# Chunk attention, top-1 MoE and a swish MLP on one core: the MoE's up-projection with its weights as the stationary operand

## The chip, the core and the metric

The kernel runs on one core of one Trainium2 chip. The engines named below are TensorE (PE, its weight loads PEld), VectorE (DVE), ScalarE (ACT), GpSimd (POOL) and SyncE (SP), which here only issues DMAs. The metric is the time of one execution on the device in microseconds (us).

## What is computed

Attention in chunks of 64, then a mixture of 8 experts in which each token goes to one, then an MLP with a swish, for 4608 tokens of width 512:

```python
def _moe_ref(x, expert_emb, tau, w1, w2):         # x [4608, 512], w1 [8, 512, 1024], w2 [8, 1024, 512]
    ...
    for e in range(E):
        mask = expert_idx == e
        ...
        h = np.maximum(x[mask] @ w1[e], 0.0)
        out[mask] = gate_w[mask, None] * (h @ w2[e])

def reference(**kwargs):
    ...
    attn_out = _attn_ref(**attn_kwargs)
    B, H, S, D = attn_out.shape
    x = np.ascontiguousarray(attn_out.transpose(0, 2, 1, 3)).reshape(B * S, H * D)
    x = _moe_ref(x=x, **moe_kwargs)
    return _moe2_ref(x=x, **moe2_kwargs)
```

The change is in the line `h = ...`: how that product is laid on PE.

## The kernel before

Three stages follow each other. The first makes attention and the router's logits for 36 tiles of 128 tokens (to about 250 us). The second sorts the tokens by expert and runs the experts over 39 tiles of at most 128 tokens of one expert each (235 to 760 us). The third is the MLP (from 764 us).

**Numbers in halves.** x, w1, h and w2 are held as a high and a low half in float16; a product takes three matmuls (high x high, high x low, low x high). w1H and w1L, w2H and w2L are the halves of the current expert's weights.

**One tile i of the expert stage.** `find(i)` and `fetch(i)` (POOL) gather the tokens' rows into xg; `turn(i)` (L867, SP) turns them with a DMA transpose into xTm: 8 blocks of 128 x 128, 4 high and 4 low, with the model's width on the partitions. `mm1(i)` is the up-projection: for each of the 4 blocks c along the width three products, each over two PSUM banks ph of 512 columns. A matmul takes a block of xTm as the stationary operand (128 x 128, loaded by a LDWEIGHTS) and moves 512 columns of w1 past it (L879): 24 matmuls, and h comes out with the tokens on the partitions. `mm1_evac(i)` then makes the two halves of h: Relu on ACT (L887), the difference on DVE (L888), one pair per bank. h has one buffer (L884). A DMA transpose on SP's queue (L892) turns h into hT, 16 blocks of 128 x 128. `mm2(i)` takes the blocks of hT as stationary operand and moves w2 (L916): 24 matmuls of 512 columns into py. `mm2_evac(i)` squares, scales and splits py on ACT and DVE (L929 to L946) and POOL scatters it to ys (L950).

**The order.** Engines run their instructions in the order of the code. In the loop over tiles 3 to 38 an iteration i is: mm1(i), turn(i+2), fetch(i+3), find(i+4), swap(i+1, 1), the matmuls of mm2(i-1), swap(i, 2), the evacuation of mm2(i-1), and one step of `dec`. So on PE mm1(i) is followed by mm2(i-1), then mm1(i+1), then mm2(i).

**swap(i, which)** (L831) is a branch on ACT and DVE that is taken where tile i is the first of an expert: four calls of `w_split` (L773), each 1024 columns, make the halves of w1 (which = 1) or w2 (which = 2) out of the staging buffers stg or stgB: ACT makes the high half (L781), DVE the low one (L786). Then SP loads the next expert's weights.

**dec** is work for the third stage that runs beside the experts: 32 blocks of w_in and w_out are loaded, decoded from float64 by ACT and four DVE instructions (up to L1166) and split by ACT (L1109) and POOL (L1110); the 16 blocks of w_in also go through sums on POOL (L1118), of which ACT's copies wait.

Of the kernel before, what the change touches and what calls it, by code (L numbers as in the profile page):

```python
# [9 lines left out]
F32 = mybir.dt.float32  # L10
F16 = mybir.dt.float16
# [3 lines left out]
AF = mybir.ActivationFunctionType  # L15
ALU = mybir.AluOpType
# [18 lines left out]
def kernel(  # L35
# [13 lines left out]
    nc = tc.nc  # L49
# [3 lines left out]
    FF = w1.shape[2]  # L53
# [3 lines left out]
    KD = DM // 128  # L57
    KF = FF // 128
# [28 lines left out]
    w1H, w1L = w1HL[:, 0], w1HL[:, 1]  # L87
# [55 lines left out]
    for t in vt:  # L143
# [15 lines left out]
        out=tri16, in_=ones16, pattern=[[1, 128]], compare_op=ALU.is_gt, fill=0.0,  # L159
# [116 lines left out]
    def steps(n):  # L276

        paused.clear()
        while n > 0 and todo:
            try:  # L280
                n -= 1
                if next(todo[0]) == "found":
                    return
            except StopIteration:
                todo.popleft()
# [147 lines left out]
    def evac_XT(t):  # L433
        xT = att.tile([128, 2 * KD, 128], F16, tag="xTa", name="xTa", bufs=2)
        xv = xT.rearrange("p (a c) k -> p a c k", a=2)
        if t >= 30:
            nc.scalar.activation(out=xv, in_=xtp, func=AF.Copy)
        else:
            nc.vector.tensor_copy(xv, xtp)  # L439
        xT_t[t] = xT  # L440
# [59 lines left out]
    def scat():  # L500
        if scats and scats[0][0] < now[0]:
            scats.popleft()[1]()
# [270 lines left out]
    def w_split(which, c, n, eng, st=stg):  # L773

        hlf, o = divmod(c * n, 2048)
        _, H_, L_ = WL[which]
        flat = slice(c * n, (c + 1) * n)
        H_ = H_.rearrange("p a f -> p (a f)")[:, flat]
        L_ = L_.rearrange("p a f -> p (a f)")[:, flat]
        src = st[hlf][:, o:o + n]  # L780
        nc.scalar.activation(out=H_, in_=src, func=AF.Copy, scale=2.0 ** W_EXP)  # L781
        if eng is nc.gpsimd:
            eng.tensor_tensor(out=src, in0=src, in1=w_pow.to_broadcast([128, n]), op=ALU.mult)
            eng.tensor_tensor(out=L_, in0=src, in1=H_, op=ALU.subtract)
        else:
            eng.scalar_tensor_tensor(  # L786
                out=L_, in0=src, scalar=2.0 ** W_EXP, in1=H_, op0=ALU.mult, op1=ALU.subtract
            )
# [19 lines left out]
    def first_split(n):  # L808
        for _ in range(n):
            c = fs_n[0]  # L810
            fs_n[0] += 1
            w_split(c // 8 + 1, c % 8, 512, (nc.vector, nc.gpsimd)[c % 2])
# [18 lines left out]
    def swap(i, which):  # L831

        if which == 1:
            flag[i] = reg(fl_i[0:1, i:i + 1], [ENG.Activation, ENG.DVE], 1)
        with tc.If(flag[i] > 0):
            for c in range(4):
                w_split(which, c, 1024, nc.vector, stage[which])
        load_next(i, which)


    mt_t, xg_t, xTm_t, hT_t = {}, {}, {}, {}
# [27 lines left out]

    ph_t = {}  # L870

    def mm1_part(i, c):
        xT = xTm_t[i]
        if c == 0:
            ph_t[i] = [ps.tile([128, 512], F32, tag="A", name="ph", bufs=2) for _ in range(2)]
        p = ph_t[i]
        for a, wt, st, sp in ((c, w1H, c == 0, False), (c, w1L, False, False), (KD + c, w1H, False, c == KD - 1)):
            for f in range(2):
                nc.tensor.matmul(p[f], xT[:, a, :], wt[:, c, f * 512:(f + 1) * 512], start=st, stop=sp)  # L879

    def mm1_evac(i):
        xTm_t.pop(i)
        p = ph_t.pop(i)
        h = mo.tile([128, 2, FF], F16, tag="h", name="h", bufs=1)  # L884
        for f in range(2):
            cc = slice(f * 512, (f + 1) * 512)
            nc.scalar.activation(out=h[:, 0, cc], in_=p[f], func=AF.Relu)  # L887
            nc.vector.scalar_tensor_tensor(  # L888
                out=h[:, 1, cc], in0=p[f], scalar=0.0, in1=h[:, 0, cc], op0=ALU.max, op1=ALU.subtract
            )  # L890
        hT = mo.tile([128, 2 * KF, 128], F16, tag="hT", name="hT", bufs=2)
        nc.sync.dma_start_transpose(hT, h.rearrange("p a f -> p (a f)"))  # L892
        hT_t[i] = hT

    def mm1(i):
        for c in range(KD):
            mm1_part(i, c)
        mm1_evac(i)

    py_t = {}  # L900

# [85 lines left out]
    for n in range(NTILE + 3):  # L987
# [46 lines left out]
        if n >= NTILE:  # L1034
            drip(6)
            mm1_part(0, n - NTILE)
    mm1_part(0, 3)
    now[0] = 2 * NTILE
    scat()
    mm1_evac(0)  # L1040
    evac_XT(NTILE - 1)
    steps(20)
    mm1_part(1, 0)
# [12 lines left out]
    while scats:  # L1056
        scat()
    mm1_part(1, 3)
    mm1_evac(1)
    steps(99)  # L1060
    find(3)
    mm2(0)
    mm1(2)
    fetch(3)
    turn(3)
# [37 lines left out]
    def big_split():  # L1103
# [3 lines left out]

        def low(f, H_, L_):
            nc.scalar.activation(out=H_, in_=f, func=AF.Copy)  # L1109
            nc.gpsimd.tensor_tensor(out=L_, in0=f, in1=H_, op=ALU.subtract)  # L1110

# [75 lines left out]
    LASTD = NSURE + 33  # L1187
    for i in range(NSURE, SURE):
        mm1(i)
        if i + 2 < SURE:  # L1190
            turn(i + 2)
# [35 lines left out]
    with tc.If(last > 0):  # L1227
        for i in range(SURE, MAXT):
            find(i)
            fetch(i)  # L1230
            turn(i)
            e = reg(pk_i[0:1, i:i + 1], [ENG.SP], NE - 1)
            for which in (1, 2):
                w_load(e, which, 0, stage[2])
                w_load(e, which, 1, stage[2])
                for c in range(4):
                    w_split(which, c, 1024, nc.vector, stage[2])
            mm1(i)
            mm2(i)
# [260 lines left out]
```

## Time and profile before

| | |
|---|---|
| time, median of 3 runs | 1485.66 us (1478.51 to 1488.81) |
| the profiled execution's own time | 1486.75 us |
| its span (first to last instruction) | 1485.0 us |
| PE busy, of the span | 1308.2 us (88%) |
| DVE, ACT, POOL busy | 853.1 (57%), 639.4 (43%), 726.6 us (49%) |
| matmuls / weight loads | 9994 / 9994 |
| mm1 (L879): 936 matmuls 128 x 512 | 220.4 us busy, 30.3 us idle before them |
| mm2 (L916): 936 matmuls 128 x 512 | 225.1 us busy, 48.5 us idle before them |
| DMA, hardware queue | 128.86 MB |

Busy time is the time in which an engine had an instruction under way; matmuls overlap, so the mean duration of one is longer than the distance between two. An idle time is put down to the event that ended it.

### The profile page before, as it was taken

What the parts mean: (1) busy time and instruction counts of PE and PEld (TensorE: products, weight loads), DVE (VectorE), ACT (ScalarE), POOL (GpSimd) and SP (SyncE); (2) the same over time, 40 slices, a digit from 0 to 9 for tenths busy, and PEclk for the clock granted to TensorE, in tenths of its full rate; (3) what the DMA queues carried; (4) which work ended last, traced back from release to release, by engine and by line L of the source; (5) the groups of instructions that cost most, each with busy time, mean ns of one, the idle gap of its engine ahead of it and who ended that gap; (6) DMA issues with size and microseconds to landing.
All of it is one profiled execution on the core that took longest, in us unless ns stands there. A gap on an engine that the chain in (4) does not pass through costs nothing. (4 is left out here: it accounts for less than half of the span.)

```text
span 1485.0 us, 26440 instructions
## 1 busy us (share of the span) xinstructions
PE 1308.2 (88%) x9994; PEld 789.0 (53%) x9994; DVE 853.1 (57%) x1681; ACT 639.4 (43%) x1125; POOL 726.6 (49%) x648
## 2 busy tenths in 40 slices
PE   6767666688878889888969999999999999999998
PEld 4656553333333334333438484848575766667573
DVE  4777868547665667666538172645546362718170
ACT  6876754125433435433426161525343342435250
POOL 1455567546655555545127263544546363627261
PEclk9997967999999899899989999999999999999999
DMA  9978766588997798888540010202020202010000
GB/s 216 227 161 191 149 111 164 145 225 191 202 244 128 191 208 216 251 211 231 108 91 2 22 37 15 44 15 44 15 44 15 43 8 50 1 50 9 29 1 29
DMA packets 277380, 160.82 MB, mean 108 GB/s; under 512 B 211048, under 2 KB 248936, under 8 KB 277232
## 3 DMA queue, kind: packets, MB, share of 16 engines
q1 hardware_dynamic: 264464, 128.86, 39.8%
q0 software_dynamic: 12768, 30.10, 6.5%
q8 instruction: 80, 1.31, 0.4%
q14 instruction: 68, 0.56, 0.1%
HBM read 89.00 MB, written 29.80 MB: 80 GB/s over the span
## 5 line engine op out<-in xcount | busy, mean ns | idle before, releaser
L1329 PEld LDWEIGHTS <-wS 128*128 128x128 f16 x3024 | 297.5, 98 | 48.1 <-issue 10.3
L916 PE MATMUL py<-w2HL,hT 128*128 128x512 f16 x936 | 225.1, 400 | 48.5 <-DMA hT<-h 45.3
L1354 POOL TENSOR_TENSOR w2HL<-z,w1HL 128x512 f16<-128x512 f32 x144 | 216.8, 1521 | 82.9 <-ACT w1HL L1353 81.4
L879 PE MATMUL ph<-w1HL,xTm 128*128 128x512 f16 x936 | 220.4, 392 | 30.3 <-DMA xTm<-xg 15.5
L916 PEld LDWEIGHTS <-hT 128*128 128x128 f16 x936 | 94.2, 102 | 176.1 <-DMA hT<-h 53.8
L879 PEld LDWEIGHTS <-xTm 128*128 128x128 f16 x936 | 92.9, 100 | 151.3 <-issue 34.2
L1449 POOL DMA_INDIRECT out_dram<-y,idc x36 | 35.5, 985 | 235.8 <-ACT y L1448 194.2
L1347 ACT ACTIVATE z<-z 128x512 f32<-128x512 f32 x144 | 88.4, 629 | 107.9 <-DVE z L1344 55.5
L950 POOL DMA_INDIRECT ys<-y,idx_y x39 | 39.0, 1000 | 168.2 <-ACT wo L1109 40.6
L846 POOL DMA_INDIRECT mt<-mtab,idx_g x78 | 91.3, 1170 | 30.5 <-issue 18.9
L1350 DVE TENSOR_TENSOR z<-stgB,z 128x512 f32<-128x512 f32 x108 | 105.2, 1000 | 0.0
L1444 PEld LDWEIGHTS <-w2HL 128*128 128x128 f16 x576 | 56.3, 98 | 68.0
L1443 PEld LDWEIGHTS <-w1HL 128*128 128x128 f16 x576 | 56.3, 98 | 67.0
L1442 PEld LDWEIGHTS <-w1HL 128*128 128x128 f16 x576 | 56.3, 98 | 67.0
L1353 ACT ACTIVATE w1HL<-z 128x512 f16<-128x512 f32 x144 | 87.0, 625 | 8.4 <-DVE z L1350 8.4
L888 DVE SCALAR_TENSOR_TENSOR h<-ph,h 128x512 f16<-128x512 f32 x78 | 50.1, 683 | 64.1 <-ACT h L887 64.1
L417 POOL TENSOR_TENSOR x<-x,sx_all 128x512 f32<-128x512 f32 x33 | 34.3, 1041 | 91.4 <-ACT PT L364 29.0
L887 ACT ACTIVATE h<-ph 128x512 f16<-128x512 f32 x78 | 42.1, 591 | 79.5 <-DMA hT<-h 44.3
L929 ACT ACTIVATE ysq<-py 128x512 f16<-128x512 f32 x39 | 23.2, 594 | 117.5 <-PE py L916 93.2
L1166 DVE SCALAR_TENSOR_TENSOR d_f<-raw_o,d_t 128x512 int32<-128x512 int32 x32 | 69.2, 2161 | 3.4 <-DVE d_t L1163 0.5
L334 PE MATMUL sp<-kuT,quT 64*64 64x64 f32 x1152 | 29.8, 252 | 41.6 <-DVE xTa L439 29.8
L1375 DVE TENSOR_TENSOR stgB<-stgB,pb 128x512 f32<-128x512 f32 x28 | 19.1, 684 | 81.6 <-PE pb L1329 75.6
(277 smaller groups left out, 2743.6 us busy)
## 6 DMA issues: line engine op xcount, KB each, us to landing
stg<-in_moe_w_dram SPq DMA_DIRECT2D x14, 1024.0 KB
stgB<-in_moe_w_dram SPq DMA_DIRECT2D x14, 1024.0 KB
vt<-in_v_dram SPq DMA_DIRECT2D x64, 144.0 KB
xs<-xr SPq DMA_DIRECT2D x36, 256.0 KB
raw_o<-in_moe_w_in_dram SPq DMA_DIRECT2D x16, 512.0 KB
raw_o<-in_moe_w_out_dram SPq DMA_DIRECT2D x16, 512.0 KB
ku<-in_k_dram SPq DMA_DIRECT2D x12, 512.0 KB
qu<-in_q_dram SPq DMA_DIRECT2D x12, 512.0 KB
```

Of the source, the lines that this page charges most:

```text
L846: nc.gpsimd.indirect_dma_start(out=mt_t[i][a][:, :], out_offset=None, in_=mtab[a][:, :], in_offset=bass.IndirectOffsetOnAxis(ap=idx_g[:, i ...
L879: nc.tensor.matmul(p[f], xT[:, a, :], wt[:, c, f * 512:(f + 1) * 512], start=st, stop=sp)
L916: nc.tensor.matmul(p, hT[:, a, :], wt[:, c, :], start=st, stop=sp)
L1166: nc.vector.scalar_tensor_tensor(out=fi, in0=hi, scalar=-(1 << 31), in1=t, op0=ALU.bitwise_and, op1=ALU.bitwise_or)
L1329: nc.tensor.matmul(dst, wS[a][:, o, kc, fs], rhs(b, kc), start=first and ab == 0 and kc == 0 and n == 0, stop=(kc == 1 and n == 2), skip_g ...
L1347: nc.scalar.activation(out=z, in_=z, func=AF.Sigmoid, scale=1.702 * 2.0 ** -G_EXP)
L1350: nc.vector.tensor_tensor(out=z, in0=c, in1=z, op=ALU.mult)
L1353: nc.scalar.activation(out=dst[0], in_=z, func=AF.Copy)
L1354: nc.gpsimd.tensor_tensor(out=dst[1], in0=z, in1=dst[0], op=ALU.subtract)
L1442: nc.tensor.matmul(p, gT[0][:, h, c, tt], wo[0][:, c, :], start=(c == 0), stop=False)
L1443: nc.tensor.matmul(p, gT[0][:, h, c, tt], wo[1][:, c, :], start=False, stop=False)
L1444: nc.tensor.matmul(p, gT[1][:, h, c, tt], wo[0][:, c, :], start=False, stop=(c == KG - 1))
```

## The change

The operands of mm1 change places. A block of w1 (128 of the width x 128 of the 1024) is the stationary operand and the 128 tokens of xTm move past it. The result comes out with the 1024 on the partitions, already in the layout of hT, so that Relu and the difference write hT straight away. h, its buffer and its DMA transpose go. The loop runs over 8 blocks f of the 1024, for each over c and the three products: 96 matmuls of 128 columns, each with a weight load. Four blocks f share a PSUM bank; the pair of evacuations of a bank is issued when its four blocks are done. The split of w1 is cut into other quarters: two blocks c by half of the 1024, in the order in which the new loop wants them. Its line numbers and the names of the buffers are otherwise as before (mm1's matmul is L888, mm2's L921, turn L872, Relu L895, the difference L896).

```diff
@@ w_split
-        flat = slice(c * n, (c + 1) * n)
-        H_ = H_.rearrange("p a f -> p (a f)")[:, flat]
-        L_ = L_.rearrange("p a f -> p (a f)")[:, flat]
-        src = st[hlf][:, o:o + n]
+        if which == 1 and n == 1024:
+            k, f = slice(c % 2 * 2, c % 2 * 2 + 2), slice(c // 2 * 512, c // 2 * 512 + 512)
+            H_, L_ = H_[:, k, f], L_[:, k, f]
+            src = st[c % 2].rearrange("p (a f) -> p a f", a=2)[:, :, f]
+        else:
...
-    def mm1_part(i, c):
+    def mm1_part(i, q):
+
         xT = xTm_t[i]
-        if c == 0:
-            ph_t[i] = [ps.tile([128, 512], F32, tag="A", name="ph", bufs=2) for _ in range(2)]
-        p = ph_t[i]
-        for a, wt, st, sp in ((c, w1H, c == 0, False), (c, w1L, False, False), (KD + c, w1H, False, c == KD - 1)):
-            for f in range(2):
-                nc.tensor.matmul(p[f], xT[:, a, :], wt[:, c, f * 512:(f + 1) * 512], start=st, stop=sp)
-
-    def mm1_evac(i):
-        xTm_t.pop(i)
-        p = ph_t.pop(i)
-        h = mo.tile([128, 2, FF], F16, tag="h", name="h", bufs=1)
-        for f in range(2):
-            cc = slice(f * 512, (f + 1) * 512)
-            nc.scalar.activation(out=h[:, 0, cc], in_=p[f], func=AF.Relu)
...
-        hT = mo.tile([128, 2 * KF, 128], F16, tag="hT", name="hT", bufs=2)
-        nc.sync.dma_start_transpose(hT, h.rearrange("p a f -> p (a f)"))
-        hT_t[i] = hT
+        if q == 0:
+            ph_t[i] = [ps.tile([128, 4, 128], F32, tag="A", name="ph", bufs=2) for _ in range(2)]
+            hT_t[i] = mo.tile([128, 2 * KF, 128], F16, tag="hT", name="hT", bufs=2)
+        p, hT = ph_t[i][q // 2], hT_t[i]
+        for f in (2 * q, 2 * q + 1):
+            fs = slice(f * 128, (f + 1) * 128)
+            for c in range(KD):
+                for wt, a in ((w1H, c), (w1H, KD + c), (w1L, c)):
+                    nc.tensor.matmul(
+                        p[:, f % 4], wt[:, c, fs], xT[:, a, :],
+                        start=(c == 0 and a == 0 and wt is w1H), stop=(c == KD - 1 and wt is w1L),
+                    )
+        if q % 2 == 0:
+            return
+        hi, lo = (hT[:, o + q // 2 * 4:o + q // 2 * 4 + 4] for o in (0, KF))
+        nc.scalar.activation(out=hi, in_=p, func=AF.Relu)
+        nc.vector.scalar_tensor_tensor(out=lo, in0=p, scalar=0.0, in1=hi, op0=ALU.max, op1=ALU.subtract)
...
     def mm1(i):
-        for c in range(KD):
-            mm1_part(i, c)
-        mm1_evac(i)
+        for q in range(4):
+            mm1_part(i, q)
```

PE's queue at the start of mm1 in an iteration of the loop, before. The names are out<-moving,stationary operand's tile for a matmul; what an instruction waits for stands in brackets, by the engine or DMA queue that signals it.

```order
L879 LDWEIGHTS xTm [waits DVE_49,DMAHW2_49]
L879 MATMUL ph<-w1HL,xTm 128x512 [waits Activation_49]
L825 UNCONDITIONAL_BRANCH
L835 UNCONDITIONAL_BRANCH
L825 UNCONDITIONAL_BRANCH
L879 LDWEIGHTS xTm
L879 MATMUL ph<-w1HL,xTm 128x512 [waits DVE_49]
L879 LDWEIGHTS xTm
L879 MATMUL ph<-w1HL,xTm 128x512 [waits DVE_49]
```

And the same place in the changed kernel.

```order
L888 LDWEIGHTS w1HL [waits DMAHW2_49,Activation_49]
L888 MATMUL ph<-xTm,w1HL 128x128 [waits DVE_49]
L888 LDWEIGHTS w1HL
L888 MATMUL ph<-xTm,w1HL 128x128
L840 UNCONDITIONAL_BRANCH
L830 UNCONDITIONAL_BRANCH
L888 LDWEIGHTS w1HL [waits DVE_49]
L888 MATMUL ph<-xTm,w1HL 128x128
L888 LDWEIGHTS w1HL
L888 MATMUL ph<-xTm,w1HL 128x128
```

In both the first matmul waits for ACT and for DVE (the weight split and the PSUM bank); what moved is that the weights now come in by the load, and that the wait for DVE's low half stands at the third matmul.

PE's queue where mm1 ends and mm2 of the tile before begins, before:

```order
L879 LDWEIGHTS xTm
L879 MATMUL ph<-w1HL,xTm 128x512
L916 LDWEIGHTS hT [waits DMAHW0_49]
L916 MATMUL py_4878<-w2HL,hT 128x512 [waits Activation_49]
L916 LDWEIGHTS hT
L916 MATMUL py_4878<-w2HL,hT 128x512 [waits DVE_49]
```

And in the changed kernel:

```order
L888 LDWEIGHTS w1HL
L888 MATMUL ph<-xTm,w1HL 128x128
L921 LDWEIGHTS hT
L921 MATMUL py_5082<-w2HL,hT 128x512 [waits Activation_49]
L921 LDWEIGHTS hT
L921 MATMUL py_5082<-w2HL,hT 128x512 [waits DVE_49]
```

The wait for the DMA queue that brings hT is gone; the load of hT has no wait of its own, since mm1 ahead of it waited already for ACT and DVE behind tile i-1's evacuation. The waits left are for the halves of w2.

SP's queue in an iteration before the loads of an expert's weights, before:

```order
L835 UNCONDITIONAL_BRANCH
L892 DMA_TRANSPOSE hT<-h 128x16x128 [waits DMAHW0_49,DVE_49]
L867 DMA_TRANSPOSE xTm<-xg 128x8x128 [waits DMAHW1_49,DMAHW5_49,DMASW2_49,PE_49]
L762 TENSOR_LOAD nf_i
L762 ISA x2
```

And in the changed kernel:

```order
L1101 DMA raw_o_4584<-in_moe_w_in_dram 128x1024 [waits DMAHW3_49,DVE_49,Activation_49]
L872 DMA_TRANSPOSE xTm<-xg 128x8x128 [waits DMAHW2_49,DMAHW4_49,DMASW2_49,PE_49]
L840 UNCONDITIONAL_BRANCH
L762 TENSOR_LOAD nf_i
L762 ISA x2
```

The transpose of h is gone, and with it SP's wait for DVE ahead of the transpose of xg.

## Rows read from the trace of the kernel before

**Rows 1.** The page's 40 slices of the span: PE's busy share in tenths

```profile
PE   6767666688878889888969999999999999999998
```

**Rows 2.** Busy us (instructions) of each engine in a stretch, granted clock, DMA share, GB/s

```profile
300.00:760.00 460.00, 395.62 (x1704) 170.52 (x1705) 282.60 (x538) 182.23 (x309) 229.43 (x226) 0.94 0.82 196
```

**Rows 3.** PE's groups by line, 300 to 760: busy, mean ns, idle before, releasers

```profile
L916 PE MATMUL py<-w2HL,hT 128*128 128x512 f16 x864 | 208.8, 402 | 46.5 <-DMA hT<-h 45.3 <-SPq L1227 1.0
L879 PE MATMUL ph<-w1HL,xTm 128*128 128x512 f16 x840 | 194.4, 388 | 19.7 <-DMA xTm<-xg 6.3 <-DVE h L888 6.1 <-ACTq L835 3.5
```

**Rows 4.** Waits, 300 to 760: total us, times, longest us

```profile
PE py L916 <- DMA hT<-h: 45.3, 16, 6.5
...
ACT h L887 <- DMA hT<-h: 44.3, 12, 6.1
```

**Rows 5.** PE in order of time: start, length, line, operation, count, idle before and releaser

```profile
304.29 7.83 PE L879 MATMUL ph<-w1HL,xTm 128*128 128x512 f16 x24 [6.31 <-DMA xTm<-xg]
...
372.88 7.04 PE L916 MATMUL py<-w2HL,hT 128*128 128x512 f16 x24 [2.73 <-DMA hT<-h]
...
506.67 5.35 PE L916 MATMUL py<-w2HL,hT 128*128 128x512 f16 x24 [0.54 <-DMA hT<-h]
...
566.20 5.34 PE L879 MATMUL ph<-w1HL,xTm 128*128 128x512 f16 x24
...
576.56 5.34 PE L879 MATMUL ph<-w1HL,xTm 128*128 128x512 f16 x24
...
610.90 8.11 PE L916 MATMUL py<-w2HL,hT 128*128 128x512 f16 x24 [3.86 <-DMA hT<-h]
...
748.06 5.35 PE L916 MATMUL py<-w2HL,hT 128*128 128x512 f16 x24 [3.67 <-DMA hT<-h]
754.42 5.35 PE L916 MATMUL py<-w2HL,hT 128*128 128x512 f16 x24 [1.02 <-SPq L1227]
```

**Rows 6.** All engines in order of time: a w1 split, an evacuation and its transpose

```profile
499.44 4.63 DVE L786 SCALAR_TENSOR_TENSOR w1HL<-stg,w1HL 128x1024 f16<-128x1024 f32 x4
...
597.00 1.27 DVE L888 SCALAR_TENSOR_TENSOR h<-ph,h 128x512 f16<-128x512 f32 x2
...
598.87 8.99 SPq L892 DMA_TRANSPOSE hT<-h  x1
```

**Rows 7.** Router transposes, logits: in order of time; then ns min/median/max by line

```profile
103.38 0.61 PE L431 MATMUL sp<-ident,xr 128*128 128x128 f16 x8 [0.32 <-DVE si_all L405]
103.38 0.43 PEld L431 LDWEIGHTS <-xr 128*128 128x128 f16 x7 [0.30 <-issue]
103.77 0.31 PEld L454 LDWEIGHTS <-xTa 128*128 128x128 f16 x8
...
L431 PEld LDWEIGHTS <-xr x288: 95/98/152, 34.4 to 245.3; 128*128 128x128 f16 x144
L431 PE MATMUL sp<-ident,xr x288: 216/219/314, 34.8 to 245.4; 128*128 128x128 f16 x144
```

**Rows 8.** PE in order of time in the third stage, 256 moving columns, a load each

```profile
780.78 1.47 PE L1329 MATMUL pc<-yT,wS 128*128 128x256 f16 x12
782.10 1.47 PE L1329 MATMUL pd<-yT,wS 128*128 128x256 f16 x12
```

**Rows 9.** ACT in order of time, a heavy step of dec

```profile
449.80 0.60 ACT L929 ACTIVATE ysq<-py 128x512 f16<-128x512 f32 x1 [5.76 <-PE py L916]
...
460.20 0.63 ACT L1109 ACTIVATE wS<-d_f 128x512 f16<-128x512 f32 x1 [2.49 <-POOL d_f L1118]
```

**Rows 10.** PE in order of time: mm1 behind a wait for ACT or DVE

```profile
364.53 5.63 PE L879 MATMUL ph<-w1HL,xTm 128*128 128x512 f16 x24 [2.08 <-DVE h L888]
...
462.19 7.31 PE L879 MATMUL ph<-w1HL,xTm 128*128 128x512 f16 x24 [2.13 <-ACTq L835]
...
516.01 7.81 PE L879 MATMUL ph<-w1HL,xTm 128*128 128x512 f16 x24 [3.99 <-DVE h L888]
...
530.32 5.63 PE L879 MATMUL ph<-w1HL,xTm 128*128 128x512 f16 x24 [1.32 <-ACTq L835]
```

More of the change, by code (lines that the diff above doesn't have):

```diff
@@ L776, in w_split @@
         _, H_, L_ = WL[which]
-        flat = slice(c * n, (c + 1) * n)
-        H_ = H_.rearrange("p a f -> p (a f)")[:, flat]
-        L_ = L_.rearrange("p a f -> p (a f)")[:, flat]
-        src = st[hlf][:, o:o + n]
+        if which == 1 and n == 1024:
[3 more added lines that the diff above has]
+        else:
+            flat = slice(c * n, (c + 1) * n)
+            H_ = H_.rearrange("p a f -> p (a f)")[:, flat]
+            L_ = L_.rearrange("p a f -> p (a f)")[:, flat]
+            src = st[hlf][:, o:o + n]
         nc.scalar.activation(out=H_, in_=src, func=AF.Copy, scale=2.0 ** W_EXP)
@@ L870 @@
     ph_t = {}
-    def mm1_part(i, c):
+    def mm1_part(i, q):
         xT = xTm_t[i]
-        if c == 0:
-            ph_t[i] = [ps.tile([128, 512], F32, tag="A", name="ph", bufs=2) for _ in range(2)]
-        p = ph_t[i]
-        for a, wt, st, sp in ((c, w1H, c == 0, False), (c, w1L, False, False), (KD + c, w1H, False, c == KD - 1)):
-            for f in range(2):
-                nc.tensor.matmul(p[f], xT[:, a, :], wt[:, c, f * 512:(f + 1) * 512], start=st, stop=sp)
-    def mm1_evac(i):
-        xTm_t.pop(i)
-        p = ph_t.pop(i)
-        h = mo.tile([128, 2, FF], F16, tag="h", name="h", bufs=1)
-        for f in range(2):
-            cc = slice(f * 512, (f + 1) * 512)
-            nc.scalar.activation(out=h[:, 0, cc], in_=p[f], func=AF.Relu)
-            nc.vector.scalar_tensor_tensor(
-                out=h[:, 1, cc], in0=p[f], scalar=0.0, in1=h[:, 0, cc], op0=ALU.max, op1=ALU.subtract
-            )
-        hT = mo.tile([128, 2 * KF, 128], F16, tag="hT", name="hT", bufs=2)
-        nc.sync.dma_start_transpose(hT, h.rearrange("p a f -> p (a f)"))
-        hT_t[i] = hT
+        if q == 0:
[15 more added lines that the diff above has]
+        nc.vector.scalar_tensor_tensor(out=lo, in0=p, scalar=0.0, in1=hi, op0=ALU.max, op1=ALU.subtract)
+        if q == 3:
+            xTm_t.pop(i)
+            ph_t.pop(i)
     def mm1(i):
-        for c in range(KD):
-            mm1_part(i, c)
-        mm1_evac(i)
+        for q in range(4):
+            mm1_part(i, q)
     py_t = {}
@@ L1039 @@
     scat()
-    mm1_evac(0)
     evac_XT(NTILE - 1)
@@ L1058 @@
     mm1_part(1, 3)
-    mm1_evac(1)
     steps(99)
```

## The prediction

> **What bounds the kernel now.** I read the busy table by stage first, to find where TensorE (PE) is not the bound; then the waits of that stage; then PE's instructions in order of time, to price each wait; last the rows from which the new matmuls are priced.
>
> The change sits in the expert stage, which ends in the 21st of the 40 slices (37 us each); from there on PE is nearly full [rows 1] and nothing of the change is left, so only the stretch up to there can move. In it (300 to 760) PE is busy 395.6 of 460 us at a granted clock of 0.94, while DVE (283), POOL (229) and ACT (182) are far from full [rows 2]. PE's idle time there stands before the two matmul groups: 46.5 us before the down-projection (L916), nearly all of it for the transposed h, and 19.7 us before the up-projection (L879) [rows 3]. The list of waits says how often: 16 waits of PE for hT, 45.3 us, the longest 6.5; ACT stands 44.3 us behind the same DMA, because h has one buffer [rows 4].
>
> What a tile costs without a wait is seen where PE runs through: mm1 starts at 566.20 and 576.56, so mm1 and mm2 take 10.36 us, 5.18 each [rows 5]. That is 24 matmuls in 5.18 us, 215.8 ns per 512 columns. The loop from mm1 of tile 4 (304.29) to the end of mm2 of tile 38 (754.42 + 5.35 = 759.8) takes 455.5 us for 35 tiles; at 10.36 it would be 362.6. So 93 us are lost to waits and to what follows a wait: after some of them the 24 matmuls take 7 to 8 us and not 5.34, at a lower clock (372.88: 7.04, 610.90: 8.11) [rows 5]. Over the 16 mm2 groups behind an hT wait the excess over 5.34 adds up to 16.4 us; the first of them is at 372.88, the last at 748.06, and not all have one (506.67: 5.35). With 1.0 us more before the last mm2 (754.42), the DMA of h costs 45.3 + 16.4 + 1.0 = **62.7 us**. The first eight of the 16, up to 506.67, hold 20.7 us of the idle time and 6.4 of the excess: 27 us in tiles 4 to 20, and 36 in the rest.
>
> Why it is late: for one of the worst, DVE ends h at 598.3, SP issues the transpose at 598.87 and is held 9 us in the issue, and PE starts at 610.90, 12.6 us after h was ready [rows 5, 6]. What covers it, mm2 of the tile before and mm1 of the next, is 10.4 us less the time of evacuation.
>
> **The change, part by part.**
>
> *The DMA goes.* Minus 62.7 us of waits and slow clock, plus whatever is late next. Per tile, 512 KB of DMA go too; no term for that, since the only other long DMA wait of PE in the loop is xTm at tile 4 (304.29), before the first transpose that PE waits for.
>
> *mm1 becomes 96 matmuls of 128 columns, each with its own weight load.* The columns are as many as before (24 x 512). The question is whether a weight load hides behind 128 columns. The nearest rows are the transposes of the router, also 128 columns with a load each: eight take 0.61 us of which the last takes 0.219, so (0.61 - 0.219) / 7 = 55.9 ns from start to start, and seven loads take 0.43 us, 55 ns apart. With 16 columns the loads come 30 ns apart ((0.31 - 0.098) / 7, eight in 0.31) [rows 7]. With 256 columns, in the long stretch of the last stage, 12 take 780.78 to 782.10, 110 ns each, as good as 256 columns alone (half of 215.8) [rows 8]. So a load takes about 30 ns of the array's side and is hidden behind 128 columns at 54 to 56 ns: 96 x 55.9 = 5.37 us per tile, +0.19 us. Lower bound: 96 x 53.9 = 5.18, no cost. Upper bounds: load and matmul one after the other, 30 + 56 = 86 ns; and the load's whole recorded time, 98 ns [rows 7]. I take 55.9, since it is the same shape; the doubt is that it was seen in runs of eight and not of 96.
>
> *The Trainium skill speaks against this.* The page "TensorE: Matmul & The Clock Gate", section "Back-to-back issue gap", gives about 81 ns per matmul for a sustained stream of loads and 128-column matmuls, and 131 ns for 512 columns. The trace disagrees with the second (215.8 ns) and, in runs of eight, with the first (55.9). By the page's 81 a tile would cost 2.6 us more and the sum would be about 1,500; by the rows it is +0.19 us.
>
> *Evacuation writes hT directly.* Same two ACT and two DVE instructions per tile, same 128x512. The first pair can start when half of mm1 is done. That looks like slack, but PE doesn't get it: mm1 of the next tile waits, with its first weight load and third matmul, until ACT and DVE have passed the branch of the weight swap, which stands in both queues behind the second pair. The gate is as before; only some 0.6 us shorter.
>
> *What is late next.* With hT out of the way, mm1(i+2) needs ACT and DVE past tile i+1 within mm1 + mm2 = 10.55 us of the end of mm2(i-1). Four things hold them longer, all in the trace now:
> - While w_in is decoded, every fourth iteration holds ACT by three copies that wait for POOL in turn: from Square at 449.80 to the last copy at 460.20, the Relu behind it, and PE restarts at 462.19 [rows 9, 10]. That is 12.4 us; about 1.7 to 2 are left over 10.55. Four times, one of them with a weight split ahead, where PE waits 3.99 us now (516.01) [rows 10]: 6 + 4 = 10 us.
> - The iteration after a w1 split: 2.08 us at 364.53, 1.32 at 530.32 [rows 10]; three times, 4.5 us.
> - Iterations that split w2: DVE ends h at 598.3 [rows 6], when mm1 could start at 576.56 + 2 x 10.36 = 597.3; 1 to 2 us, hidden by the hT wait today. Five times, 10 us.
> - The new order of the w1 split: mm1 meets the second split after 6 matmuls (0.34 us) and not after 1.3 us, and a split on DVE takes 1.16 us (four in 4.63 [rows 6]), so up to 0.8 us at 7 swaps; half of it, 3 us.
>
> Together 27 to 28 us, of which today's trace already pays about half; and some 4 us of slow clock behind them (at 516.01 mm1 takes 7.81). The first stretch (tiles 4 to 20) so keeps most of its waits under another name, the second loses nearly all of its 36.
>
> *SP.* turn(i+2) and the weight loads no longer queue behind the transpose of h. They were in time before; nothing.
>
> *Tiles 0 to 2.* 3 x 0.19, and the first part of mm1(0) needs all four K chunks of w1: 1 us. Together 1.6.
>
> **The sum.** 304.3 + 35 x 10.55 (369.3) + 2.5 (slow clock at tile 4: 7.83 for 5.34) + 27.5 + 4 = 707.6, against 759.8: minus 52. Plus 1.6 ahead of it: -50.6. Tail and last stage as before. The profiled execution took 1486.75 us (span 1485.0), 1.1 above the median of the three runs (1485.66); I give back 2 us for waits that fall together: **1438 us**.
>
> **The rivals.**
> *(a) Loads and matmuls don't overlap in a long stream: slower.* For it: only runs of eight were seen, and a load's record is 98 ns. Against it: 256 columns hide it fully. At 86 ns mm1 takes 8.26 us, a tile 13.44; the loop 304.3 + 35 x 13.44 + 3 = 777.7, +18; tiles 0 to 2 +9: 1514. At 98 ns: 14.59 per tile, 1557. It decides from about 82 ns on: there 35 x 13.05 eats the whole gain and 1 per cent more.
> *(b) The late engines take over everything in the first stretch.* The 27 us there come back as ACT and DVE waits: 1465. For it: 449.80 to 462.19. Against it: 20.7 of the 45.3 us of hT waits are there, and not all fall beside a heavy iteration.
> *(c) Nothing is late next.* Earlier Relu also pulls ACT's chain forward (ACT no longer waits 44.3 us for h's buffer): the 28 + 4 us go too, about 1408; half of it, 1422.
>
> **How the numbers follow.** Forecast with its own spread of about 15 us: 0.62. (a) 0.14. (b) 0.10. (c) 0.14. The range runs from 1420 (half of (c)) to 1480: it takes in (b) and a rate of up to 70 ns (+47 us, of which the waits cover some), and leaves out (a) and the end of (c), together 0.2. A measurement of this kernel can tell about 1 per cent from no change. Faster by over 1 per cent (under 1471): forecast, (c) and most of (b), 0.79; within 1 per cent: 0.07; slower: 0.14.
>
> **What would show it.** In the profile after: 3744 matmuls of 128x128 from L888, the 96 of a tile in 5.4 to 5.6 us; no hT<-h DMA; waits of PE at L888 for ACT and DVE of 20 to 30 us in the loop and almost none at mm2; from 566 on the equivalent of tile 24 onwards gapless but for the w2 splits; mm2 of tile 38 ending near 710. If the 96 take 8 us with PE never idle, the rate step is wrong and (a) holds; if mm1 keeps its 5.4 us and PE waits 50 us for ACT or DVE, the step on what is late next is wrong.

## The result, and the profile after

The changed kernel takes **1434.9 us** (median of 4 runs, 1432.5 to 1437.0) where the kernel before takes 1483.6 us on the same chip (4 runs, 1478.5 to 1488.8): a ratio of **0.967, interval 0.963 to 0.971**. In a later comparison (e9 below) it was 1441.6 against 1489.0 us, 0.969 (0.967 to 0.971). 1438 us was forecast.

Three views of the changed kernel's profiled execution (1432.45 us, span 1430.7), which answer to [rows 1], [rows 2] and [rows 3]. The page's 40 slices, of 35.8 us each:

```profile
PE   6776666788989899999899999999999999999998
```

Busy us and instructions of each engine in the expert loop (PE, PEld, DVE, ACT, POOL), then granted clock, DMA share and GB/s:

```profile
300.00:709.00 409.00, 385.98 (x4208) 279.74 (x4205) 281.98 (x542) 182.61 (x309) 224.16 (x224) 0.97 0.64 171
```

PE's two matmul groups between 298 and 706 us: busy us, mean ns | idle us before, releasers:

```profile
L888 PE MATMUL ph<-xTm,w1HL 128*128 128x128 f16 x3360 | 205.6, 225 | 26.7 <-DMA xTm<-xg 6.8 <-DVE hT L896 6.5 <-ACT w1HL L786 5.1
L921 PE MATMUL py<-w2HL,hT 128*128 128x512 f16 x864 | 192.2, 379 | 0.0
```

PE does the work that took 395.6 of 460 us in 386.0 of 409. The granted clock went from 0.94 to 0.97, the DMA share from 0.82 to 0.64. The idle time before mm2 (L921, L916 before) is gone, all 46.5 us of it. The idle time before mm1 (L888) has grown from 19.7 to 26.7 us, and 6.8 of that stands ahead of tile 4, where it was 6.3. PE's waits in the same stretch, total us, times, longest, for [rows 4]:

```profile
PE ph L888 <- DMA xTm<-xg: 6.8, 1, 6.8
PE ph L888 <- DVE hT L896: 6.5, 4, 3.8
PE ph L888 <- ACT w1HL L786: 5.1, 2, 2.6
PE ph L888 <- DVE w1HL L791: 3.3, 5, 1.1
PE ph L888 <- DVEq L840: 3.1, 8, 0.4
PE ph L888 <- ACTq L840: 1.8, 1, 1.8
```

Behind tile 4, all that is left are waits of mm1 for ACT and DVE, 19.9 us (20 to 30 were forecast), where the list of before had 45.3 us for the DMA. (L840 is the branch of the weight swap in ACT's and DVE's queues.) In order of time, for [rows 5] and [rows 10]: start, length, line, operation, count, idle before:

```profile
298.08 8.23 PE L888 MATMUL ph<-xTm,w1HL 128*128 128x128 f16 x96 [6.85 <-DMA xTm<-xg]
...
345.67 0.29 PE L888 MATMUL ph<-xTm,w1HL 128*128 128x128 f16 x2 [2.56 <-ACT w1HL L786]
346.93 0.51 PE L888 MATMUL ph<-xTm,w1HL 128*128 128x128 f16 x6 [0.97 <-DVE w1HL L791]
348.06 6.71 PE L888 MATMUL ph<-xTm,w1HL 128*128 128x128 f16 x88 [0.62 <-DVE w1HL L791]
...
359.79 5.52 PE L888 MATMUL ph<-xTm,w1HL 128*128 128x128 f16 x96
365.15 5.34 PE L921 MATMUL py<-w2HL,hT 128*128 128x512 f16 x24
371.37 0.27 PE L888 MATMUL ph<-xTm,w1HL 128*128 128x128 f16 x2 [0.88 <-DVE hT L896]
...
494.00 0.27 PE L888 MATMUL ph<-xTm,w1HL 128*128 128x128 f16 x2 [3.79 <-DVE hT L896]
494.66 7.05 PE L888 MATMUL ph<-xTm,w1HL 128*128 128x128 f16 x94 [0.39 <-DVEq L840]
...
508.32 0.27 PE L888 MATMUL ph<-xTm,w1HL 128*128 128x128 f16 x2 [1.42 <-DVE hT L896]
...
524.77 5.34 PE L921 MATMUL py<-w2HL,hT 128*128 128x512 f16 x24
...
605.17 5.42 PE L888 MATMUL ph<-xTm,w1HL 128*128 128x128 f16 x94 [0.39 <-DVEq L840]
...
695.35 10.52 PE L921 MATMUL py<-w2HL,hT 128*128 128x512 f16 x48
```

The 96 matmuls of a tile run from 359.79 to 365.15: 5.36 us, 55.8 ns each, with a weight load apiece. Stops come in the first half of the loop, in mm1's first eight matmuls, and behind four of the long ones the rest of that mm1 runs at a lower granted clock: 0.68 to 0.75 over those stretches, where 360 to 371 us has 1.00 (6.71 and 7.05 us, where 88 and 94 matmuls take 5.1 and 5.4). From 520 us on there is next to nothing.

Below, **the loop** is the time from the first matmul of mm1(4) to the end of the last mm2. Here it is 298.08 to 705.87, **407.8 us, where it was 455.5**. It came out within 0.4 us in a second execution of each kernel (455.3 and 407.4, e4 and e9), which is better than the whole time does: the stage ahead of it varies by up to 14 us between the profiles. So the experiments are read by it, against 407.6 us, the mean of the two profiles of the kernel after. A table for the loop, summed over PE's groups in order of time:

| us | before | after |
| --- | --- | --- |
| matmuls at full rate (35 mm1, 36 mm2) | 367.8 | 374.1 |
| idle behind waits | 59.2 | 19.9 |
| groups longer than at full rate (slow clock) | 24.2 | 10.1 |
| rest: filling and draining at each stop | 4.3 | 3.7 |
| loop | 455.5 | 407.8 |

### The profile page after: what moved, and what is told of

It reads as the page before. It is cut to its first block, busy times and chain, and to the rows that moved or that the text cites. A ratio compares the mean times of both kernels' runs of the same rounds, so it can differ in the third digit from the quotient of the medians.

```text
span 1430.7 us, 31954 instructions
## 1 busy us (share of the span) xinstructions
PE 1296.3 (91%) x12802; PEld 912.8 (64%) x12802; DVE 852.4 (60%) x1681; ACT 639.0 (45%) x1125; POOL 723.1 (51%) x648
## 4 chain that ended last, share of the span: by engine, by line
PE 50%; DMA 3%; issue 1%; POOL 0%; DVE 0%; ACT 0%; POOLq 0%; DVEq 0%; ACTq 0%
PE pb L1332 6%; PE pd L1332 6%; PE pa L1332 6%; DMA xg<-xs,mt 3%; PE pc L1332 3%; PE gb L1332 3%; PE pa L1447 2%; PE pa L1445 2%; PE pa L1446 2%; PE pd L1447 2%; PE pd L1445 2%; PE pd L1446 2%; PE pb L1446 2%; PE pb L1447 2%; PE pb L1445 2%; PE gb L1445 1%
## 5 line engine op out<-in xcount | busy, mean ns | idle before, releaser
L888 PE MATMUL ph<-xTm,w1HL 128*128 128x128 f16 x3744 | 233.7, 227 | 35.9 <-DMA xTm<-xg 16.0
L888 PEld LDWEIGHTS <-w1HL 128*128 128x128 f16 x3744 | 227.1, 102 | 50.7 <-issue 21.1
L921 PE MATMUL py<-w2HL,hT 128*128 128x512 f16 x936 | 208.4, 379 | 0.8 <-POOL w2HL L789 0.8
L921 PEld LDWEIGHTS <-hT 128*128 128x128 f16 x936 | 89.8, 98 | 102.5 <-issue 1.1
L851 POOL DMA_INDIRECT mt<-mtab,idx_g x78 | 87.6, 1123 | 30.4 <-issue 19.4
L1445 PEld LDWEIGHTS <-w1HL 128*128 128x128 f16 x576 | 56.4, 98 | 67.0
L1446 PEld LDWEIGHTS <-w1HL 128*128 128x128 f16 x576 | 56.4, 98 | 67.0
L896 DVE SCALAR_TENSOR_TENSOR hT<-ph,hT 128x512 f16<-128x512 f32 x78 | 50.9, 682 | 43.6 <-ACT hT L895 42.9
L895 ACT ACTIVATE hT<-ph 128x512 f16<-128x512 f32 x78 | 44.3, 590 | 51.9 <-PE ph L888 51.6
```

Of the source, the lines that this page charges most:

```text
L851: nc.gpsimd.indirect_dma_start(out=mt_t[i][a][:, :], out_offset=None, in_=mtab[a][:, :], in_offset=bass.IndirectOffsetOnAxis(ap=idx_g[:, i ...
L888: nc.tensor.matmul(p[:, f % 4], wt[:, c, fs], xT[:, a, :], start=(c == 0 and a == 0 and wt is w1H), stop=(c == KD - 1 and wt is w1L),)
L921: nc.tensor.matmul(p, hT[:, a, :], wt[:, c, :], start=st, stop=sp)
L1445: nc.tensor.matmul(p, gT[0][:, h, c, tt], wo[0][:, c, :], start=(c == 0), stop=False)
L1446: nc.tensor.matmul(p, gT[0][:, h, c, tt], wo[1][:, c, :], start=False, stop=False)
```

## The experiments

Each ratio is to the kernel before on the same chip: e1 to e4 ran on one chip (before: 1495.3 us), e5 to e8 on a second (1491.4), e9 to e11 on a third (1489.0), e12 on the first again (1491.0).

### e1: the turning DMA and its wait put back

The kernel after, but ACT and DVE write into a tile h of one buffer, a DMA transposes that, and mm2 reads what the DMA wrote (turned once too often, so y is not the reference's).

```diff
-            hT_t[i] = mo.tile([128, 2 * KF, 128], F16, tag="hT", name="hT", bufs=2)
+            hT_t[i] = mo.tile([128, 2 * KF, 128], F16, tag="h", name="h", bufs=1)
...
             ph_t.pop(i)
+            turned_h = mo.tile([128, 2 * KF, 128], F16, tag="hT", name="hT", bufs=2)
+            nc.sync.dma_start_transpose(turned_h, hT.rearrange("p a t -> p (a t)"))
+            hT_t[i] = turned_h
```

> The changed kernel with one part undone: ACT and DVE write their halves into a one-buffer tile, a DMA transpose of the old size turns it into the two-buffer hT, and mm2 reads that (what it computes is another matrix of the same size; only the timing counts). mm1 keeps its 96 matmuls of 128 columns. Theory (the wait for the DMA was the cost, the 128-column form costs 0.18 us per tile): all of the gain goes, 1483 to 1497 us, with about 16 waits of PE for hT. Rival (a good part of the gain comes from the new form of mm1, its earlier evacuation or its split order): between 1445 and 1475 us.

Measured: 1507.4 us, ratio 1.011 (1.006 to 1.016), loop 463.7 us. PE's waits in the loop begin

```profile
PE py L924 <- DMA hT<-h: 39.5, 13, 6.8
```

So all of the gain hangs on the DMA, and the rest of the change costs: the loop is 8.2 us longer than before. 35 x 0.18 us for the 128-column matmuls is 6.3 of it. The time lies above the 1483 to 1497 us that were expected.

### e2: the DMA without a reader

The kernel after, plus the same transpose into a tile that nobody reads.

```diff
             ph_t.pop(i)
+            extra = mo.tile([128, 2 * KF, 128], F16, tag="h", name="extra", bufs=1)
+            nc.sync.dma_start_transpose(extra, hT.rearrange("p a t -> p (a t)"))
```

> The changed kernel plus a DMA transpose of hT, of the old size and on the old queue, into a tile that nobody reads. Theory (the wait costs, not the DMA's load on the queues): 1433 to 1441 us. Rival (the transposes slow the other transfers, and their absence was a part of the gain): 1450 us or more, with longer waits for xTm, raw_o or the staged weights.

Measured: 1482.0 us, ratio 0.992 (0.989 to 0.996), loop **438.2 us, 30.6 more than the kernel after**, though PE never waits for that DMA. The rival held. The medians say the same: beside the kernel before on its chip e2 keeps 13.3 us of a gain that was 48.6 and 47.4 (e9) without the transpose. PE's first waits in the loop, and three places in order of time:

```profile
PE ph L888 <- DMA xTm<-xg: 16.7, 5, 7.6
PE ph L888 <- ACT w1HL L786: 8.5, 3, 4.8
PE ph L888 <- issue: 6.7, 13, 1.0
```

```profile
611.58 0.39 PE L888 MATMUL ph<-xTm,w1HL 128*128 128x128 f16 x2 [4.80 <-ACT w1HL L786]
...
686.47 7.43 PE L888 MATMUL ph<-xTm,w1HL 128*128 128x128 f16 x96 [2.25 <-DMA xTm<-xg]
...
702.40 4.53 PE L888 MATMUL ph<-xTm,w1HL 128*128 128x128 f16 x74 [3.32 <-DMA xTm<-xg]
...
708.73 1.11 PE L888 MATMUL ph<-xTm,w1HL 128*128 128x128 f16 x17 [1.01 <-issue]
```

The same transposes that were in time in the kernel after, xTm's, come late (four more waits), a swap's split of w1 comes late (4.80 us), and PE stops inside mm1 for 0.2 to 1 us without waiting for anything that the profile shows ("issue"). For the stop at 611.58 the rows show the way: SP's queue stands 9.58 us in the extra transpose, and ACT's split of w1 waits for SP.

```profile
595.50 9.58 SPq L901 DMA_TRANSPOSE extra<-hT  x1
```

```profile
610.47 3.90 ACT L786 ACTIVATE w1HL<-stg 128x1024 f16<-128x1024 f32 x4 [8.24 <-SPq L830]
```

### e3: the wait without its reader

The kernel before, but mm2 takes a constant as its weights in the array in place of the turned h. h is still made and turned; y is not the reference's.

```diff
-                nc.tensor.matmul(p, hT[:, a, :], wt[:, c, :], start=st, stop=sp)
+                nc.tensor.matmul(p, ones16, wt[:, c, :], start=st, stop=sp)
```

> The kernel before, in which mm2 takes a constant 128x128 block as its stationary operand, so that it waits for no transpose; h is still made and transposed, and ACT still waits for h's one buffer (the experts' result is left out). Theory: PE's waits of 45 us and most of the 16 us of slow clock behind them go, about half of that comes back as waits for ACT and DVE, of which those for h's buffer are a part the changed kernel doesn't have: 1435 to 1455 us. Rival (the wait only hid other waits of the same size): 1470 us or more.

Measured: 1475.9 us, ratio 0.989 (0.986 to 0.993), loop 435.3 us, 20.0 less than before. The wait for hT is gone from PE, and here is what stands in its place, PE's waits from 315 to 751 us and ACT's for the DMA:

```profile
PE ph L879 <- ACTq L835: 14.6, 5, 4.6
PE ph L879 <- DVE h L888: 14.4, 8, 5.2
PE ph L879 <- DMA xTm<-xg: 12.1, 3, 6.4
```

```profile
ACT h L887 <- DMA hT<-h: 71.0, 13, 10.2
```

ACT waits 71.0 us for the DMA to let go of h's one buffer (44.3 before, [rows 4]), and PE waits for ACT and DVE. It also waits 5.7 us for xTm within the loop (the other 6.4 stand ahead of it), which the kernel before never does. The 1435 to 1455 us that I expected were missed, and the time is in the rival's range. So this kernel doesn't price PE's wait by itself: its waits point to a second way in which the DMA holds PE, through h's buffer and ACT.

### e4: the kernel before, again

Unchanged.

> The kernel before, unchanged, profiled a second time. The first mm1 started at 235.0 us before and at 228.8 after, ahead of anything that the change touches. Theory (the start of the first stage differs from execution to execution): the first mm1 of this one lies anywhere from 227 to 240 us, and the loop from tile 4 to tile 38 takes 453 to 458 us again. Rival (the change moved the first stage): 234 to 236 us.

Measured: 1491.4 us, ratio 1.000 (0.997 to 1.004), first mm1 at 236.7 us, loop 455.3. So by its loop the kernel before is here what it was in its first profile.

### e5: the unread DMA issued last

As e2, but behind all else that SP issues in an iteration.

```diff
         if i < LASTD:
             next(dec, None)
+        extra = mo.tile([128, 2 * KF, 128], F16, tag="h", name="extra", bufs=1)
+        nc.sync.dma_start_transpose(extra, hT_t[i].rearrange("p a t -> p (a t)"))
```

> The kernel after, plus a transposing DMA of hT (512 KB written) into a tile that nobody reads, as in e2_dma_no_wait, but issued at the end of the iteration, behind turn(i+2), the loads of staged weights and the loads of raw blocks on SP's queue, where nothing is left for it to hold up. Theory Q, the order on SP's queue: in e2_dma_no_wait SP stood at the transpose until DVE had written hT, and turn and the staged loads came late behind it; then this one comes back to the kernel after, ratio to before 0.965 to 0.975. Theory L, the load that the transpose puts on the 16 DMA engines: the place doesn't matter, and the ratio stays at 0.985 to 1.00, with the loop (first matmul of mm1(4) to the last of mm2(38)) at 430 to 445 us where the kernel after has 407.8.

Measured: 1477.1 us, ratio 0.988 (0.983 to 0.993), loop 440.2 us, as slow as e2. That is what theory L expects, but a new wait clouds it. Of ACT's waits:

```profile
ACT hT L895 <- DMA extra<-hT: 56.6, 12, 12.4
```

Issued later, the transpose holds hT's buffers longer, and ACT waits for them (6.2 us in e2). The order on SP's queue isn't told apart from the load by this run.

### e6: a plain copy in its place

As e2, but a plain copy of hT, the same 512 KB.

```diff
+            extra = mo.tile([128, 2 * KF, 128], F16, tag="h", name="extra", bufs=1)
+            nc.sync.dma_start(out=extra, in_=hT)
```

> The kernel after, plus a plain DMA copy of hT into a tile that nobody reads, at the place of e2_dma_no_wait's transpose: the same bytes, the same wait of SP's queue for DVE, but rows copied as they stand instead of turned. If it is the form of the transfer (many small packets, a large share of the engines' time) that costs, this is 0.965 to 0.975 of before, a loop of 408 to 415 us. If the bytes or the place in SP's queue cost, it stays at 0.985 to 1.00, a loop of 430 to 445 us.

Measured: 1458.7 us, ratio 0.977 (0.972 to 0.982), loop 418.9 us: 11.3 more than after, of which the "issue" pauses hold 7.5. Between both expectations, nearer to the first. The issues on SP's queue, ns min/median/max, of e2 and then of e6:

```profile
L901 SPq DMA_TRANSPOSE extra<-hT x39: 1652/3778/9582, 256.5 to 746.8; - x39
```

```profile
L901 SPq DMA_DIRECT2D extra<-hT x39: 465/486/692, 256.6 to 725.0; - x39
```

And the hardware queue's line on the page of e2, e6 and the kernel after: packets, MB, time of the packets as a share of 16 engines' span (1477.2, 1457.0 and 1430.7 us):

```profile
q1 hardware_dynamic: 264464, 128.86, 42.4%
```

```profile
q1 hardware_dynamic: 188960, 128.86, 38.5%
```

```profile
q1 hardware_dynamic: 183344, 108.41, 33.2%
```

A transpose holds SP's queue for 3.8 us in the median, up to 9.6, where the copy holds it for 0.5. For the same 20.4 MB it makes 81,120 packets and the copy 5,616. In time of the engines that is (0.424 x 1477.2 - 0.332 x 1430.7) / 39 = 3.9 us per transpose and, in the same way, 2.2 us per copy. Both stand at the same place on SP, behind the same wait for DVE. So neither the bytes nor that wait carry most of e2's 30.6 us; the turning does, by its hold on SP (seen at one stop of e2), its packets, or both, and how the 30.6 us divide these runs don't tell. The transpose also reads hT and so holds its buffers: ACT waits for that once in e2, 6.2 us at 708.03, and no wait of PE follows.

The Trainium skill says on its page "Advanced Engine Details and Errata", section "X-Bar Transpose (TRN2)", that transposing DMAs are as fast as regular ones. For this one, from SBUF to SBUF beside weight loads, the rows above disagree.

### e7: the old order of w1's split

The kernel after with the pieces of the split of w1 as before.

```diff
-        if which == 1 and n == 1024:
+        if False:
```

> The kernel after, with the split of w1 in the order of before (ACT, DVE, DVE for one block of 128 rows at a time, over all of F) in place of the new one by pairs of blocks of f. The prediction had 3 us of loss in the new order's late pieces and none in a wait for the old one. My theory: mm1 with its tokens moving wants all of the first f block's rows of w1 early, the old order gives the last of these later, so each binding swap of w1 costs some 1 us more: 2 to 13 us slower than the kernel after, ratio to before 0.968 to 0.977, and the waits for ACT or DVE w1HL in the first matmuls of mm1 grow from 13 us. Rival: swaps are hidden by mm2 of the tile before, no change, 0.965 to 0.969.

Measured: 1453.8 us, ratio 0.973 (0.968 to 0.978), loop 416.1 us, 8.5 more than after. Three of PE's waits in the loop:

```profile
PE ph L888 <- DVE w1HL L791: 6.7, 11, 1.1
PE ph L888 <- DVEq L840: 6.0, 9, 0.8
PE ph L888 <- issue: 4.3, 9, 1.0
```

The waits for DVE's half of the split rise from 3.3 to 6.7 us and those at the branch from 3.1 to 6.0, as the theory has it; the wait for hT falls from 6.5 to 3.1. 4.3 us are "issue" pauses, of which neither profile of the kernel after has any; without them the order is worth some 4 us of the loop. The ratio alone, beside 0.969 (0.967 to 0.971), doesn't settle it.

### e8: the evacuation late

The kernel after with both pairs of evacuations behind the 96 matmuls.

```diff
-        if q % 2 == 0:
+        if q < 3:
             return
```

(and the ACT and DVE lines in a loop over both banks).

> The kernel after, with the first pair of evacuations (ACT and DVE on the first bank of ph) behind all 96 matmuls of mm1 instead of in their middle. Theory of the prediction, step 3: the early pair buys nothing while mm1(i+1) is held by ACT's and DVE's place in their queues, and mm2(i-1), 5.2 us, covers both pairs: 0 to 6 us slower than the kernel after, ratio to before 0.967 to 0.972. Rival: in the heavy iterations, where ACT and DVE come late, each of the second pairs comes 1.3 us later and mm1(i+1) with it: up to 20 us slower, 0.975 to 0.982.

Measured: 1453.4 us, ratio 0.973 (0.968 to 0.978), loop 413.7 us, 6.1 more than after, 3.8 of it "issue" pauses. PE's wait for hT is 6.8 us, as after (6.5). By the loop without the pauses the early pair buys 2 us or so, as forecast; the ratio beside 0.969 doesn't settle that either.

### e9: the kernel after, again

Unchanged.

> The kernel after, unchanged, beside the kernel before on the same chip. In its first profile the stage ahead of the loop, whose instructions the change doesn't touch, ended 6.2 us earlier than in the kernel before (first matmul of mm1 at 228.8 us against 235.0), while the seven kernels of the experiments so far had it at 236.7 to 243.0. Theory A: that stage's length varies by itself from chip to chip or execution to execution; then the first mm1 is at 234 to 243 us here, mm1(4) to the last mm2 again takes 406 to 410 us, and the ratio to before is 0.969 to 0.976. Theory B: it belongs to the changed program; then the first mm1 is at 227 to 231 us again, and the ratio 0.963 to 0.970.

Measured: 1441.6 us, ratio 0.969 (0.967 to 0.971), first mm1 at 237.4 us, loop 407.4. Theory A: the 6.2 us ahead of the loop in the first profile are not the change's. By the medians the change is worth 47.4 us here and 48.6 in the first comparison, by the loops 47.7.

### e10: the sums spread

The kernel after; one of the two sums of the third block of dec goes to the fourth, and the fourth's to the next step.

```diff
+            if old and b % 4 == 0:
+                pb, f0, f3 = old.pop()
+                pk, pc = divmod(pb // 4, 2)
+                minus(f0, f3, f0)
+                low(f0, *(w[:, T4, pk, pc * 512:(pc + 1) * 512] for w in wS))
...
-                minus(f[0], f[2], f[0])
-                put(T2, f[0])
...
-                minus(f[0], f[3], f[0])
-                put(T4, f[0])
+                minus(f[0], f[2], f[0])
+                put(T2, f[0])
+                old[:] = [(b, f[0], f[3])]
```

> A candidate that may beat the kernel after: the same, but in the decomposition that runs beside the loop (dec) the two sums and four copies of one heavy step in four are spread over neighbouring steps, so that no step has more than one sum on POOL and two copies. The heavy steps are where mm1's waits for ACT, DVE and their queues are left (13 to 15 us with the slow clock behind them). My theory: 1 to 8 us faster than the kernel after, the loop at 400 to 407 us. Rival: the waits move to the next swap, which comes every fourth tile too, no change, 407 to 410 us.

Measured: **1436.1 us** (1435.3 to 1438.9), ratio 0.964 (0.962 to 0.966), beside 1441.6 (1439.9 to 1445.7) for the kernel after on the same chip: 5.5 us faster, and no run of one overlaps the other. The loop is 400.7 us, 6.7 less. It beats both kernels. PE's waits in the loop:

```profile
PE ph L888 <- ACTq L840: 5.6, 3, 2.5
PE ph L888 <- DVE hT L896: 5.1, 4, 3.0
PE ph L888 <- DVEq L840: 4.0, 10, 0.6
```

The 5.1 us behind ACT's half of the split (345.67 and its like) are gone, and 3.8 came back at ACT's branch; all waits together fall by 2.4. The rest of the gain is the clock behind the stops: the excess of slow groups adds up to 4.7 us, where it is 9.4 in e9.

### e11 and e12: the price of the sums, after and before

dec's sums on POOL left out, in the kernel after (e11) and in the kernel before (e12).

```diff
-            nc.gpsimd.tensor_tensor(out=o, in0=x, in1=y, op=ALU.subtract)
+            pass
```

> The kernel after without the sums that dec has on POOL (its differences of splits are left out, so the decomposed weights, and the output, are not the reference's). It prices step 4 of the prediction, what is late next: if ACT and DVE come late because they stand behind POOL's sums, the waits of mm1 in tiles 7 to 20 go (w1HL 2.6 and 2.6 us, ACTq 1.8, hT 3.8 and 1.4) with the slow clock behind them: 8 to 20 us faster than the kernel after, loop 388 to 400 us. Rival: they stand behind ACT's own copies and the swap's split, and nothing of it goes, loop 404 to 410 us.

> The kernel before without the sums that dec has on POOL (its differences of splits are left out, so the output is not the reference's), the counterpart of e11_no_sums, where leaving them out of the kernel after took 18.2 us from the loop (407.4 to 389.2). My theory, step 4 of the prediction: in the kernel before, PE's wait for the turned h covers most of the lateness that the sums put on ACT and DVE, so they are worth little there: the loop 443 to 451 us where the kernel before has 455.4, ratio 0.990 to 0.998. Rival: the sums cost the same in both kernels and nothing was uncovered by the change: the loop 434 to 440 us, ratio 0.985 to 0.989.

Measured, e11: 1423.3 us, 18.3 less than the kernel after on the same chip, loop 389.2 us, 18.2 less; ratio to before 0.957 (0.954 to 0.960). e12: 1481.9 us, ratio to before 0.992 (0.989 to 0.996), loop 456.7 us, where e4 had 455.3. Its profiled execution is the slowest of its five; by the ratio over all of them the sums are worth 11 us in the kernel before (7 to 16). PE's waits in the loop, of e4 and then of e12:

```profile
PE py L916 <- DMA hT<-h: 43.8, 16, 7.2
PE ph L879 <- ACTq L835: 5.5, 2, 3.4
...
PE ph L879 <- ACT w1HL L781: 4.5, 2, 2.4
PE ph L879 <- DVE h L888: 3.9, 3, 3.1
```

```profile
PE py L916 <- DMA hT<-h: 62.5, 18, 7.7
...
PE ph L879 <- DVE h L888: 1.0, 1, 1.0
```

In the profiled loop of the kernel before, the waits for ACT and DVE went as well, 13 us of them, and the wait for hT grew by 18.7: nothing came of it. After the change, the same edit brings 18 us. By the profile the cover is even fuller than I expected; by the ratio it is as expected, and partial.

## Why the prediction was right, and where it was not

**The sum.** A slip is in it. The loop from mm1(4) on holds 35 mm1 but 36 mm2, because mm2(3) comes behind mm1(4); "35 x 10.55" leaves one mm2, 5.2 us, out, and so the 93 us that the kernel before loses are 87.7. Rightly added the forecast is 1443 us, not 1438. That the slip brought it nearer to 1434.9 is luck; the range, 1420 to 1480, holds either way. In lost time it was 2.5 + 27.5 + 4 = 34.0 us after the change; measured are 33.7 (407.8 - 374.1).

**The DMA goes.** The size held: 59.2 + 24.2 us of idle time and slow clock became 19.9 + 10.1, 53.4 less, and the 128-column matmuls take 6.3 back. The halves held too: up to mm2(21), 524.77 us after, the loop lost 54.7 us before and loses 31.6 now, "most of its waits under another name"; behind it 32.8 became 1.9. So rival (b), by which the first half gains nothing, is out by 23 us, and (c), by which nothing is late next, by most of the 31.6.

The reason was half of one. "512 KB of DMA per tile go too; no term for that" is wrong: put back with no reader, the transpose takes 30.6 of the 47.7 us (e2). The step failed because it looked only at which waits the load caused in the kernel before; there PE's wait for hT covered the late xTm and the late split of w1 that come to light in e2, and xTm in e3 as well (5.7 us). The wait taken away alone brings 20.0 us and not 60 (e3, where the DMA still holds h's buffer). The sum came out since wait and load went together, and the price was taken from waits that both made.

**96 matmuls with a load each.** 55.9 ns were taken from runs of eight; 55.8 are measured in runs of 96, and rival (a) is out. The Trainium skill's 81 ns for such a stream (the page "TensorE: Matmul & The Clock Gate", section "Back-to-back issue gap") isn't what this kernel shows; its 131 ns for 512 columns isn't either (5.18 us / 24 = 215.8, before and after).

**Evacuation.** The gate was the one forecast, ACT's and DVE's place in front of the branch: after the change the stops stand at mm1's first load or after its second matmul (494.00, x2). e8 puts the early pair at some 2 us of the loop.

**What is late next.** The right engines, in the right half, with sizes wrong that cancel.
- The heavy steps were put at 10 us and their slow clock at 4. From one mm2's start to the next, four tiles take 16.85, 17.51, 14.73 and 16.68 us instead of 10.54: **23.6 us** with the clock. Two of the four meet a split of w1, not one, and on ACT the split stands behind the copies that wait for POOL:

```profile
339.94 0.63 ACT L1112 ACTIVATE wS<-d_f 128x512 f16<-128x512 f32 x1 [4.02 <-POOL d_f L1121]
343.06 0.63 ACT L1112 ACTIVATE wS<-d_f 128x512 f16<-128x512 f32 x1 [2.49 <-POOL d_f L1121]
...
344.55 3.89 ACT L786 ACTIVATE w1HL<-stg 128x1024 f16<-128x1024 f32 x4
```

- PE's stop behind that one is 345.67: 2.56, 0.97, 0.62, then 6.71 us for 88 matmuls. The trace of before had a stop at the same tile, which the prediction left out:

```profile
351.10 0.59 PE L879 MATMUL ph<-w1HL,xTm 128*128 128x512 f16 x2 [2.73 <-ACT w1HL L781]
```

- e11 shows that POOL's sums are the cause of 17.0 of the 28.9 us which the loop loses from mm2(4) to mm2(21).
- The iterations that split w2 were put at 10 us and those after a w1 split at 4.5. A tile right after a w1 split now stops only where a heavy step meets it (494.00; 359.79 doesn't). Two tiles behind a split of w2 there is a short stop, six times: 1.6, 1.1 and 2.1 us with all else up to mm2(21) (371.37 and 508.32 are the first and third), then 0.6, 0.7 and 0.6 (605.17 is one), **6.8 us** in all. Behind 524.77 they are all that is lost, **1.9 us**. The step took DVE's end of h at 598.3 as if DVE would come as late without the DMA; ACT's 44 us behind h's buffer ([rows 4]) likely made part of that lateness; no run here takes that apart. That such a chain moves forward was in rival (c), and there it happened; in the first half POOL's sums hold most of the rest (e11).
- The new order of w1's split at 3 us: 5 waits, 3.3 us, all but 0.3 of it inside the heavy steps above; the old order would be worse by some 4 us (e7, less its pauses).

With tile 4 (2.7 us, forecast 2.5) and the one late piece outside a heavy step (0.4), that makes 33.5 of the 33.7 us.

**SP.** "In time before; nothing" was too quick: in e2 xTm and a split of w1 come late behind the transpose, the split visibly by its hold on SP (8.24 us of ACT's time), xTm by that or by the engines' load. That gain is in the 30.6 us above.

**Tiles 0 to 2.** Forecast +1.6; from the first mm1 to mm1(4) it is 69.3 us before and after. Nothing.

**The ends.** The changed profile's stage ahead of the loop was 6.2 us shorter than before, which e9 doesn't repeat: it isn't the change's. The 2 us of give-back are too small to see.

## What to carry to other kernels

A DMA that is taken out can give back two things, the wait for it and its hold on the queue and the engines, and here the wait list of the kernel before showed only the first; price the second by adding the transfer where nobody reads it. Where one long wait stands in each iteration, the engines behind it can look in time and not be: the sums are worth nothing in the profiled loop of before, 11 us (7 to 16) by its medians (e12), and 18 after (e11), so the trace of after is the place to look for the next edit (e10). Weights standing and tokens moving by 128 columns cost 3.5% of a matmul's time here, 55.8 ns against 53.9, which is cheap if it spares a transpose.

## What the hardware showed that was not expected

- A transposing DMA from SBUF to SBUF that nobody waits for made the loop 30.6 us longer (35 of them in it), a plain copy of the same bytes 11.3 us (e2, e6).
- In e2 and e5, at DMA shares of 0.92 and 0.90 in the loop, PE paused within mm1 for 6.7 and 10.9 us in all, in stops of 0.2 to 1.1 us, and the profile shows nothing that it waited for. e6 to e8 have 7.5, 4.3 and 3.8 us of it, though, at shares of 0.76, 0.62 and 0.63, e1 1.2 at 0.82, and the kernel after, e10 and e11 none. e1 and e2 ran on one chip, e5 to e8 on another, e9 to e11 on a third. A late supply of PE's instructions is a candidate that no run tests. Whether the pauses go with the load, the chip, or the program isn't settled, and 2 to 4 us of e7's and e8's difference hang on it.
- The stage ahead of the loop, with the same instructions in all, put the first mm1 at 228.8 to 243.0 us, while the loop of either kernel repeated to 0.4 us.
